# Turning the attention's output by transposing DMAs from two fp16 parts, instead of by TensorE from fp32

## The chip, the cores and the metric

One Trainium2 chip, of which the kernel uses one core. The metric is the device time of one execution in microseconds (us); lower is better. Engines are called as in the profile: PE (TensorE) with its weight loads PEld, DVE (VectorE), ACT (ScalarE), POOL (GpSimd), SP (the engine that issues the DMAs; SPq in the timeline).

## The reference

```python
# x: 2048 rows of 640; 32 heads of 20; window of 256
xn = layernorm(x)
q, k, v = split(xn @ wqkv)                      # 640 -> 3 * 640
p = softmax(where(0 <= i - j < 256, q @ k.T * 20 ** -0.5, -1e9))
s = (p @ v) @ wo                                # attention, then the last projection
h = relu(xn @ w1 + b1) ** 2                     # 640 -> 1536
g = silu(h @ w2 + b2)                           # 1536 -> 640
return x + s * g
```

Products are made in fp16: a matrix is split into a high part and a low part (the rounding rest), and three products (high by high, high by low, low by high) are added.

## The kernel before, in words

Three stages. The first normalises x, turns it, makes v and the first q and k. The second is the attention, with the MLP mixed in. The third ("the last stage" here) multiplies the attention's output with wo, by silu of the MLP's output y, and adds x.

The attention is a loop over 269 steps: 16 pairs of heads by 16 query tiles of 128 rows, plus a lag. In each step TensorE makes scores for the maxima (sps, `scores`) and, ten steps later, transposed scores into a PSUM tile of which there is only one (stps, `scores_t`). ACT takes the exponential (p, `exps`), POOL masks it with two selects (L627, L629), ACT makes its high part (ph, `high`), DVE the low part (pl, `low`), and TensorE multiplies both with v (ops, `values`). Every four steps a group of 4 query tiles for one pair of heads is done, 64 groups in all: ACT copies ops out (osb, `normed`), DVE takes a reciprocal (rs), POOL adds two halves (on, L667) and multiplies by rs (L670), and SP stores the result to the DRAM tile of that group of rows (o_0 to o_3). These three parts of `normed` are spread: osb at the end of a step, the addition in the next step, and the multiplication late in that same step.

Into the gaps TensorE gets other work from a generator (`filler`), with a budget per step: q and k of the later pairs, then `hidden_unit` (hps, with relu and hh on ACT, sq on DVE and a subtraction to hh on POOL as its evacuation), `out_unit` (yps, stored to y), and last `out_filler`, the last stage. Evacuations are put in a list and run by `flush()`, once a step.

The order on each engine is that of the program text: the schedule is written out by hand. All DMAs go through SP, one queue, in order; each also waits for the one issued eight places before it. mrow is a small transfer to qs (the maxima's rows, 2 KB), which stps of later steps need.

The last stage has 8 units of 256 rows. `load` brings the unit's rows of o and y back (ob, yb); `transposes` turns ob on TensorE (otp: 10 transposes of 128x128 fp32), ACT and DVE split the result to fp16 parts (oT); then 60 products (wops), their evacuation on DVE (`finish`) and the store. Unit 0's transposes are placed in the attention's last steps, each other unit's inside the unit ahead of it. Large tiles share a pool of ten (`bigp`), used in turn.

Of the kernel before, what the change touches and what calls it, by code (L numbers as in the profile page):

```python
# [7 lines left out]
F32 = mybir.dt.float32  # L8
# [6 lines left out]
P = 128  # L15
S = 2048
D = 640
# [41 lines left out]
def attn_mlp_kernel(ctx: ExitStack, tc, x, wqkv, wo, w1, b1, w2, b2, out):  # L59
# [23 lines left out]

    v_d = dram.tile([P, NP, NB, 4 * 2 * VW], F16, name="v_d")
    y_d = dram.tile([P, NT, D], F32, name="y")
    o_d = [dram.tile([4, P, D], F32, name=f"o_{g}") for g in range(NB)]


    ident = const.tile([P, P], F32, name="ident")
# [568 lines left out]
    def normed(p, g):  # L658
        ot = ots.pop((p, g))
        osb = at2.tile([P, 8, VW], F32, tag="osb", name="osb")  # L660
        nc.scalar.activation(osb, ot.rearrange("p a h w -> p (a h) w"), AF.Copy)

        def rest():
            rs = at2.tile([P, 8], F32, tag="rs", name="rs")
            nc.vector.reciprocal(rs, osb[:, :, VW - 1])
            on = at2.tile([P, 8, DH], F32, tag="on", name="on")
            nc.gpsimd.tensor_add(on, osb[:, :, 0:DH], osb[:, :, DH:2 * DH])  # L667

            def last():
                nc.gpsimd.tensor_mul(on, on, rs.unsqueeze(2).to_broadcast([P, 8, DH]))  # L670
                post(o_d[g].rearrange("t p d -> p t d")[:, :, 2 * DH * p:2 * DH * (p + 1)], on.rearrange("p (t h) d -> p t (h d)", t=4))
            norm.append(last)
        return rest


    early = at2.tile([P, 1], F32, tag="early", bufs=1, name="early")
    state = [0.0, 0.0, 0]
# [2 lines left out]
    def post(dst, src):  # L680
        posts.append((dst, src))
# [12 lines left out]
    def flush(upto=None):  # L694
        for f in late[:]:
            f()
        late.clear()
        while pending and (upto is None or flushed[0] < upto):
            flushed[0] += 1
            pending.pop(0)()  # L700
# [214 lines left out]
    def filler():  # L915
        groups = [(group_unit, g, b, w) for g in range(1, KC) for b in range(NB) for w in "qk"]
        hid = [[(hidden_unit, n, fc) for fc in range(NF)] for n in range(nblk)]
        mlp2 = [[(out_unit, n, tt, nh, third) for tt in range(2) for nh in range(2) for third in range(3)] for n in range(nblk)]
        first = 3 * NB
        units = groups[:first] + merge(groups[first:], hid[0])  # L920
        for n in range(nblk - 1):
            units += merge(hid[n + 1], mlp2[n])
        units += mlp2[-1]
        for u in units:
            if u == (hidden_unit, 1, 2):
                out_scales()
            if u[:3] == (hidden_unit, nblk - 1, 0):
                wo_part = queue_wo()
                shut.add("o")
            if u[:2] == (out_unit, nblk - 1):  # L930
                shut.discard("o")
                load(0)
                load(1)
            if u == (out_unit, nblk - 1, 1, 1, 1) and 0 in ld:
                yield from transposes(0)
            yield from u[0](*u[1:])
        ensure("o")
        yield from out_filler(wo_part)

    ld = {}  # L940

    def ready(u):
        return state[2] >= NP * NT - NT + 4 * (u // 2) + 3 + LAG + 5

    def load(u):
        if u in ld or u >= 2 * NB or not ready(u):
            return
        if u % 2 == 0:
            obs[u // 2] = [bigp.tile([P, KC * BT], F32, tag="big", name=f"{w}_{u // 2}").rearrange("p (u t d) -> p u t d", u=2, t=2) for w in ("ob", "yb")]
        ob, yb = (t_[:, u % 2] for t_ in obs[u // 2])  # L950
        t0 = 2 * (u % 2)
        nc.sync.dma_start(ob, o_d[u // 2][t0:t0 + 2].rearrange("t p d -> p t d"))
        nc.sync.dma_start(yb, y_d[:, 2 * u:2 * u + 2, :])
        ld[u] = (ob, yb)

    obs = {}

    def queue_wo():
        wob = [bigp.tile([P, SLOT], F16, tag="big", name=f"wo{j}") for j in range(2)]
        for c in range(KC):  # L960
            hi, lo = (lin1(wob, (2 * c + q) * D, D) for q in range(2))
            piece("o", wo[c * P:(c + 1) * P, :], lambda raw, hi=hi, lo=lo: split_s(hi, lo, raw, mlp["so"]))
        return lambda p, c: lin1(wob, (2 * c + p) * D, D)

    oT = {}

    def transposes(u):
        ob = ld[u][0]
        oT[u] = bigp.tile([P, SLOT], F16, tag="big", name=f"oT_{u}")[:, :SLOT // 2].rearrange("p (s c n) -> p s c n", s=2, c=KC)
        for c0 in range(0, KC, 2):  # L970
            cs = range(c0, min(c0 + 2, KC))
            flush(mark() - 2)
            if state[2] < 10 ** 6:
                ps = pmm.tile([P, len(cs), MT], F32, tag="mm", name="otp")
            else:
                if c0 == 2:
                    ps = pst.tile([P, 2, 4 * P], F32, tag="st", name="otp")[:, 0, :].rearrange("p (c n) -> p c n", n=MT)
                else:
                    ps = pat.tile([P, len(cs), MT], F32, tag="s", name="otp")
            for c in cs:  # L980
                for t in range(2):
                    nc.tensor.transpose(ps[:, c - c0, t * P:(t + 1) * P], ob[:, t, c * P:(c + 1) * P], ident)  # L982
                    yield 0.12

            def evac(ps=ps, c0=c0, n=len(cs)):
                split(oT[u][:, 0, c0:c0 + n], oT[u][:, 1, c0:c0 + n], ps)
            pending.append(evac)

    def out_filler(wo_part):
        xts = {}  # L990

        def load_res(t):
            xts[t] = wgt.tile([P, D], F32, tag="wraw", bufs=RAW, name="xres")
            nc.sync.dma_start(xts[t], x[t * P:(t + 1) * P, :])

        def finish(ps, sl, t2, nh, res, xt, t, yb):
            nc.vector.scalar_tensor_tensor(res[:, sl], ps, mlp["io"], yb[:, t2, sl], ALU.mult, ALU.mult)
            nc.vector.tensor_add(res[:, sl], res[:, sl], xt[:, sl])
            if t == NT - 1:
                post(out[t * P:(t + 1) * P, sl], res[:, sl])  # L1000
            elif nh:
                post(out[t * P:(t + 1) * P, :], res)

        load_res(0)
        for u in range(2 * NB):
            while u not in ld:
                load(u)
                if u not in ld:
                    yield None
            load(u + 1)  # L1010
            if u not in oT:
                yield from transposes(u)
            flush()
            yb = ld[u][1]
            nc.scalar.activation(yb, yb, AF.Silu)
            for t2 in range(2):
                t = 2 * u + t2
                xt = xts.pop(t)
                res = wgt.tile([P, D], F32, tag="ysb", name="res")
                for nh in range(2):  # L1020
                    if t2 and not nh and u + 1 in ld:
                        yield from transposes(u + 1)
                    sl = slice(nh * HALF, (nh + 1) * HALF)
                    cuts = [sl] if (t, nh) != (NT - 1, 1) else [slice(HALF, HALF + HALF // 2), slice(HALF + HALF // 2, D)]
                    for sl in cuts:
                        ps = pmm.tile([P, HALF], F32, tag="mm", name="wops")[:, 0:sl.stop - sl.start]
                        mms = []
                        for c in range(KC):
                            for op, wp in ((0, 0), (0, 1), (1, 0)):
                                mms.append((oT[u][:, op, c, t2 * P:(t2 + 1) * P], wo_part(wp, c)[:, sl]))  # L1030
                        yield from mm_group(ps, mms, 0.138)
                        if sl is not cuts[-1]:
                            pending.append(lambda ps=ps, sl=sl: finish(ps, sl, t2, nh, res, xt, t, yb))
                    if nh == 0 and t + 1 < NT:
                        load_res(t + 1)
                    load(u + 1)
                    load(u + 2)

                    pending.append(lambda args=(ps, sl, t2, nh, res, xt, t, yb): finish(*args))
# [17 lines left out]
    with tc.manual_schedule(engines={E_.PE, E_.Activation, E_.DVE, E_.Pool, E_.SP}):  # L1057
# [5 lines left out]
        for s in range(steps):  # L1063
# [34 lines left out]
                maxima(*a, sc)  # L1098
            if rows:
                rows()  # L1100
            if norm:
                norm.pop()()
            if b:
# [9 lines left out]
                high(*c, *exs.pop(c))  # L1113
            while norm:
                norm.pop()()
            fill((1 - EARLY_FILL) * per + SWING * (-1) ** (s - LAG - 3))
            if e and e[1] % 2:
                values(e[0], e[1] - 1)
# [2 lines left out]
                    norm.append(normed(e[0], e[1] // 4))  # L1121
        while norm:
            norm.pop()()
        state[2] = 10 ** 6
        for _ in fl:
            post_all()
# [26 lines left out]
```

## Time and profile before

| | |
|---|---|
| median of 3 runs | 824.12 us (823.79 to 825.47) |
| the profiled execution | 825.52 us, of which the span of the instructions is 823.8 us |
| granted TensorE clock | 1.00 |
| busy: PE, DVE, ACT, POOL | 812.3, 688.8, 646.6, 481.7 us |
| DMA | 104.51 MB, queue q1 40.9% of 16 engines' span |

A line of the timeline has the start in us, the length in us, the engine, the line of the kernel, the operation, out<-in, the shapes; in brackets the idle time before it and what ended it. A line of the stretches has the stretch and its length, then the busy us (and instructions) of PE, PEld, DVE, ACT and POOL, the granted clock, the DMA engines' mean busy share, and GB/s. Matmuls overlap, so their lengths add up to more than the time they take.

### The profile page before, as it was taken

How to read it: one execution, taken by the hardware profiler on the slowest of the kernel's cores; microseconds unless marked ns; L12 is line 12 of the kernel's file. 1: busy time of each engine (PE TensorE's matmuls, PEld its weight loads, DVE VectorE, ACT ScalarE, POOL GpSimd, SP SyncE). 2: the span in 40 equal slices, each digit the busy share in tenths (PEclk: the TensorE clock that was granted, in tenths of full speed). 3: DMA queues.
4: the chain of work that ended last, by engine and by line, in shares of the span. 5: the costliest groups of instructions: out<-in, count | busy, mean ns of one | idle time of the engine just before them, and what ended most of it. 6: DMA issues, size and time to landing. Idle time of an engine off the chain costs nothing.

```text
span 823.8 us, 24953 instructions
## 1 busy us (share of the span) xinstructions
PE 812.3 (99%) x9453; PEld 546.3 (66%) x9453; DVE 688.8 (84%) x1903; ACT 646.6 (78%) x1024; POOL 481.7 (58%) x874
## 2 busy tenths in 40 slices
PE   8999999999999999999999999999999999999998
PEld 7775563455555567777777777777777777767776
DVE  6777566888899999899989999899998999975665
ACT  5466455999899989898989989899998989893321
POOL 2000000566587788787878878888887879760000
PEclk9999999999999999999999999999999999999999
DMA  6895357764654621121222222122132231056883
GB/s 243 248 343 159 127 165 246 225 179 122 185 153 141 181 89 51 51 67 39 66 67 56 67 57 67 36 70 66 35 80 56 75 83 47 26 186 201 295 293 130
DMA packets 100641, 104.51 MB, mean 127 GB/s; under 512 B 42536, under 2 KB 73000, under 8 KB 100520
## 3 DMA queue, kind: packets, MB, share of 16 engines
q1 hardware_dynamic: 100520, 102.91, 40.9%
q8 instruction: 74, 1.21, 0.7%
q14 instruction: 47, 0.39, 0.2%
HBM read 65.67 MB, written 36.83 MB: 124 GB/s over the span
## 4 chain that ended last, share of the span: by engine, by line
PE 89%; ACT 4%; DVE 3%; DMA 2%; issue 1%; SPq 1%; POOL 0%; ACTq 0%; DVEq 0%; POOLq 0%
PE hps L705 20%; PE yps L901 19%; PE qkps L705 11%; PE ops L654 8%; PE wops L705 8%; PE sps L574 8%; PE vps L293 6%; PE stps L621 4%; PE qkps L519 3%; DMA raw<-in_A_wqkv_dram 1%; PE otp L982 1%; ACT p L626 1%; DMA wvr<-in_A_wqkv_dram 1%; PE tps L257 1%; ACT ph L634 1%
## 5 line engine op out<-in xcount | busy, mean ns | idle before, releaser
L626 ACT ACTIVATE p<-stps,ebias,esc 128x768 f32<-128x768 f32 (+2 forms) x256 | 242.2, 946 | 39.5 <-PE stps L621 32.8
L585 DVE CUSTOM_DVE_ANT_0 junk<-sps,mask 128x320 bf16<-128x320 f32 (+2 forms) x512 | 221.3, 469 | 45.7 <-PE sps L574 36.5
L640 DVE TENSOR_TENSOR pl<-p,ph 128x768 f16<-128x768 f32 (+2 forms) x256 | 245.7, 960 | 3.5 <-ACT ph L634 2.0
L627 POOL TENSOR_SCALAR_AFFINE_SELECT p<-p 128x256 f32<-128x256 f32 x256 | 174.5, 682 | 77.2 <-ACT p L626 73.6
L634 ACT ACTIVATE ph<-p 128x768 f16<-128x768 f32 (+2 forms) x256 | 203.0, 793 | 3.0 <-POOL p L629 3.0
L705 PE MATMUL hps<-xT,w 128*128 128x256 f16 x1440 | 189.5, 273 | 0.7 <-ACT relu L875 0.7
L901 PE MATMUL yps<-w,hh 128*128 128x320 f16 x1152 | 187.3, 300 | 0.0
L705 PEld LDWEIGHTS <-w 128*128 128x128 f16 x1440 | 132.4, 98 | 44.9 <-issue 25.4
L901 PEld LDWEIGHTS <-hh 128*128 128x128 f16 x1152 | 104.8, 98 | 56.2 <-issue 22.6
L705 PE MATMUL qkps<-xT,qkw 128*128 128x512 f16 x480 | 115.4, 380 | 0.0
L629 POOL TENSOR_SCALAR_AFFINE_SELECT p<-p 128x256 f32<-128x256 f32 x224 | 109.9, 491 | 0.0
L654 PE MATMUL ops<-vp,ph 128*128 128x41 f16 x1440 | 89.8, 181 | 0.0
L654 PE MATMUL ops<-vp,pl 128*128 128x41 f16 x1440 | 89.5, 180 | 0.0
L654 PEld LDWEIGHTS <-ph 128*128 128x128 f16 x1440 | 84.6, 96 | 5.1
L574 PE MATMUL sps<-ks,qs 60*64 60x320 f16 (+2 forms) x1024 | 84.0, 313 | 2.6 <-DVE mt L585 2.3
L654 PEld LDWEIGHTS <-pl 128*128 128x128 f16 x1440 | 78.9, 96 | 5.1
L590 POOL CAST mp<-mt 128x8 f16<-128x8 f32 x64 | 44.7, 698 | 57.9 <-DVE mt L585 57.4
L621 PE MATMUL stps<-qs,ks 62*64 62x320 f16 (+4 forms) x1024 | 77.5, 290 | 0.6 <-ACT p L626 0.4
L705 PEld LDWEIGHTS <-qkw 128*128 128x128 f16 x480 | 42.5, 98 | 53.7 <-issue 11.5
L879 POOL TENSOR_TENSOR hh<-sq,hh 128x256 f16<-128x256 f32 x96 | 67.2, 700 | 14.2 <-DVE sq L878 8.1
L293 PE MATMUL vps<-wv,xT 128*128 128x320 f16 x480 | 69.6, 299 | 1.3 <-DVE xT L267 0.4
L705 PE MATMUL wops<-wo,oT 128*128 128x320 f16 (+1 forms) x495 | 66.7, 295 | 0.0
(152 smaller groups left out, 977.9 us busy)
## 6 DMA issues: line engine op xcount, KB each, us to landing
raw<-in_B_w_dram SPq DMA_DIRECT2D x24, 320.0 KB
ks<-k_d SPq DMA_DIRECT2D x64, 120.0 KB
qs<-q_d SPq DMA_DIRECT2D x64, 120.0 KB
v_d<-vt SPq DMA_DIRECT2D x8, 656.0 KB
vp<-v_d SPq DMA_DIRECT2D x16, 328.0 KB
xt<-in_A_x_dram SPq DMA_DIRECT2D x16, 320.0 KB
k_d<-shm SPq DMA_DIRECT2D x20, 256.0 KB
q_d<-shm SPq DMA_DIRECT2D x20, 256.0 KB
```

Source lines behind the costliest of these rows:

```text
L293: nc.tensor.matmul(ps, xT[b][:, xp, c, t * P:(t + 1) * P], wv[wp][:, c, nh * HALF:(nh + 1) * HALF], start=n == 0, stop=n == 3 * KC - 1)
L574: nc.tensor.matmul(ps[HB * j:HB * (j + 1), :nk], qs[i][rows_, q0:q0 + HB], ks[i][rows_, k0:k0 + nk], start=True, stop=True)
L585: nc.vector.tensor_tensor_reduce(out=junk[:, :nk], in0=ps[:, :nk], in1=mk, scale=1.0 / MAX_UNIT, scalar=-3.0e38, op0=ALU.add, op1=ALU.max, ...
L621: nc.tensor.matmul(ps[HB * j:HB * (j + 1), hh, c0:c1], ks[i][rows_, kb * P + HB * j:kb * P + HB * (j + 1)], qs[i][rows_, kb * P + c0:kb * ...
L626: nc.scalar.activation(p32[:, :, :n], ps[:, :, :n], AF.Exp, scale=esc[0], bias=ebias)
L627: nc.gpsimd.affine_select(p32[:, :, 0:P], p32[:, :, 0:P], pattern=[[0, 2], [1, P]], compare_op=ALU.is_ge, fill=0.0, base=0, channel_multip ...
L629: nc.gpsimd.affine_select(p32[:, :, 2 * P:], p32[:, :, 2 * P:], pattern=[[0, 2], [-1, P]], compare_op=ALU.is_gt, fill=0.0, base=0, channel ...
L634: nc.scalar.activation(ph[:, :, :n], p32[:, :, :n], AF.Copy)
L640: nc.vector.tensor_sub(pl[:, :, :n], p32[:, :, :n], ph[:, :, :n])
L654: nc.tensor.matmul(ot[:, q % 4, hh, :], t[:, hh, (q - k) * P:(q - k + 1) * P], vp[:, k // 4, k % 4, hh, :], start=m == 1, stop=m == 2 * le ...
L705: nc.tensor.matmul(ps, a, b_, start=j == 0, stop=j == n - 1)
L901: nc.tensor.matmul(ps, hh[:, hp, tt * P:(tt + 1) * P], lin1(w2t, (2 * fc + wp) * D + nh * HALF, HALF), start=fc == 0 and j == 0, stop=fc = ...
```

## The change

The DRAM tiles for the attention's output become fp16, with a high part and a low part. After POOL's multiplication a group is put in a list (`halves`). In the next step, ahead of `exps`, ACT copies it to fp16 (onp, `halves_high`); later in that step DVE makes the low part (`halves_low`), and two stores follow instead of one. In the last stage, `load` issues two transposing DMAs for a unit (one for each part), straight to oT; `transposes` and its evacuations are gone. y's rows are loaded by `load_y`: those of units 0 to 3 at the first `hidden_unit` of the last block, 4, 5 and 6 in the last `out_unit`s, and 7 at the last stage's start. x's rows are loaded two tiles ahead instead of one.

```diff
-    o_d = [dram.tile([4, P, D], F32, name=f"o_{g}") for g in range(NB)]
+    o_d = [dram.tile([2, BT, D], F16, name=f"o_{g}") for g in range(NB)]
...
             def last():
                 nc.gpsimd.tensor_mul(on, on, rs.unsqueeze(2).to_broadcast([P, 8, DH]))
-                post(o_d[g].rearrange("t p d -> p t d")[:, :, 2 * DH * p:2 * DH * (p + 1)], on.rearrange("p (t h) d -> p t (h d)", t=4))
+                halves.append((on.rearrange("p a d -> p (a d)"), g, p))
             norm.append(last)
...
+    def halves_high():
+        on, g, p = halves.pop()
+        parts = at2.tile([P, 2, 8 * DH], F16, tag="onp", name="onp")
+        nc.scalar.activation(parts[:, 0], on, AF.Copy)
+        return on, parts, g, p
+
+    def halves_low(on, parts, g, p):
+        nc.vector.tensor_sub(parts[:, 1], on, parts[:, 0])
+        for s in range(2):
+            post(o_d[g][s].rearrange("(t p) d -> p t d", p=P)[:, :, 2 * DH * p:2 * DH * (p + 1)], parts[:, s].rearrange("p (t d) -> p t d", t=4))
...
             if u[:3] == (hidden_unit, nblk - 1, 0):
                 wo_part = queue_wo()
+                for y in range(4):
+                    load_y(y)
...
-            if u == (out_unit, nblk - 1, 1, 1, 1) and 0 in ld:
-                yield from transposes(0)
...
     def load(u):
...
-        nc.sync.dma_start(ob, o_d[u // 2][t0:t0 + 2].rearrange("t p d -> p t d"))
-        nc.sync.dma_start(yb, y_d[:, 2 * u:2 * u + 2, :])
...
+        for s in range(2):
+            nc.sync.dma_start_transpose(oT[u][:, s], o_d[u // 2][s, u % 2 * MT:(u % 2 + 1) * MT, :])
...
-                    if t2 and not nh and u + 1 in ld:
-                        yield from transposes(u + 1)
...
             if rows:
                 rows()
+            turned = halves_high() if halves else None
             if norm:
                 norm.pop()()
...
             while norm:
                 norm.pop()()
+            if turned:
+                halves_low(*turned)
```

On ACT, the 53rd of the 64 groups (in the profile before it begins at 648.81 us), from osb on. In brackets stands what an instruction waits for. Before:

```order
L661 ACTIVATE osb_13422<-ops_13305 128x328 [waits PE_49]
L626 ACTIVATE p32_13445<-stps_1667,ebias_113,esc_904 128x768 [waits DVE_49,PE_49]
L634 ACTIVATE ph_13457<-p32_13378 128x768 [waits Activation_49,Pool_49]
L626 ACTIVATE p32_13485<-stps_1667,ebias_113,esc_904 128x768 [waits DVE_49,PE_49,Activation_49]
L875 ACTIVATE relu_13499<-hps_13384,m_2_1304,m_0_1302 128x256
```

Now:

```order
L661 ACTIVATE osb_13630<-ops_13511 128x328 [waits PE_49]
L626 ACTIVATE p32_13653<-stps_1667,ebias_113,esc_904 128x768 [waits DVE_49,PE_49]
L634 ACTIVATE ph_13665<-p32_13586 128x768 [waits Activation_49,Pool_49]
L681 ACTIVATE onp_13692<-on_13651 128x160 [waits DMAHW7_49,DMAHW6_49,Pool_49]
L626 ACTIVATE p32_13694<-stps_1667,ebias_113,esc_904 128x768 [waits DVE_49,PE_49,Activation_49]
```

onp stands between ph and the next p, and waits for POOL. POOL's order in the same group, now (before, the same instructions in the same order):

```order
L667 TENSOR_TENSOR on_13651<-osb_13630 128x160 [waits Activation_49]
L627 AFFINE_SELECT p32_13653<-p32_13653 128x2x128 [waits Activation_49]
L629 AFFINE_SELECT p32_13653<-p32_13653 128x2x128
L670 TENSOR_TENSOR on_13651<-on_13651,rs_13649 128x160 [waits DVE_49,Pool_49]
L627 AFFINE_SELECT p32_13694<-p32_13694 128x2x128 [waits Activation_49]
```

The multiplication that onp reads comes behind the two selects of the p one step earlier. On SP in the last stage, before, around the loads of unit 4:

```order
L994 DMA xres_15831<-in_A_x_dram 128x640 [waits DMAHW5_49]
L952 DMA ob_2_15833<-o_2_81 128x2x640 [waits DMAHW6_49,PE_49]
L953 DMA yb_2_15834<-y_78 128x1280 [waits DMAHW7_49,PE_49]
L685 DMA out_0_dram<-res_15813 128x640 [waits DMAHW0_49,DVE_49]
L994 DMA xres_15893<-in_A_x_dram 128x640 [waits DMAHW1_49]
```

Now:

```order
L698 DMA out_0_dram<-res_15976 128x640 [waits DMAHW5_49,DVE_49]
L976 DMA_TRANSPOSE oT_2_16039<-o_2_81 128x5x256 [waits DMAHW6_49,PE_49]
L976 DMA_TRANSPOSE oT_2_16039<-o_2_81 128x5x256 [waits DMAHW7_49]
L992 DMA xres_16058<-in_A_x_dram 128x640 [waits DMAHW0_49]
L698 DMA out_0_dram<-res_16021 128x640 [waits DMAHW1_49,DVE_49]
```

Two transposing DMAs stand where one load of o and one of y stood.

More of the change, by code (lines that the diff above doesn't have):

```diff
@@ L670, in last @@
                 nc.gpsimd.tensor_mul(on, on, rs.unsqueeze(2).to_broadcast([P, 8, DH]))
-                post(o_d[g].rearrange("t p d -> p t d")[:, :, 2 * DH * p:2 * DH * (p + 1)], on.rearrange("p (t h) d -> p t (h d)", t=4))
+                halves.append((on.rearrange("p a d -> p (a d)"), g, p))
             norm.append(last)
         return rest
+    halves = []
+    def halves_high():
[7 more added lines that the diff above has]
+            post(o_d[g][s].rearrange("(t p) d -> p t d", p=P)[:, :, 2 * DH * p:2 * DH * (p + 1)], parts[:, s].rearrange("p (t d) -> p t d", t=4))
     early = at2.tile([P, 1], F32, tag="early", bufs=1, name="early")
@@ L933, in filler @@
                 load(1)
-            if u == (out_unit, nblk - 1, 1, 1, 1) and 0 in ld:
-                yield from transposes(0)
+                load_y(4)
+                load_y(5)
+            if u == (out_unit, nblk - 1, 1, 1, 2):
+                load_y(6)
             yield from u[0](*u[1:])
@@ L938, in filler, with load_y @@
         yield from out_filler(wo_part)
-    ld = {}
+    obs, ybs = {}, {}
     def ready(u):
-        return state[2] >= NP * NT - NT + 4 * (u // 2) + 3 + LAG + 5
+        return state[2] >= NP * NT - NT + 4 * (u // 2) + 3 + LAG + 6
+    def load_y(u):
+        if u not in ybs and u < 2 * NB:
+            if u % 2 == 0:
+                obs["y", u // 2] = bigp.tile([P, KC * BT], F32, tag="big", name=f"yb_{u // 2}").rearrange("p (u t d) -> p u t d", u=2, t=2)
+            ybs[u] = obs["y", u // 2][:, u % 2]
+            nc.sync.dma_start(ybs[u], y_d[:, 2 * u:2 * u + 2, :])
     def load(u):
-        if u in ld or u >= 2 * NB or not ready(u):
+        if u in oT or u >= 2 * NB or not ready(u):
             return
         if u % 2 == 0:
-            obs[u // 2] = [bigp.tile([P, KC * BT], F32, tag="big", name=f"{w}_{u // 2}").rearrange("p (u t d) -> p u t d", u=2, t=2) for w in ("ob", "yb")]
-        ob, yb = (t_[:, u % 2] for t_ in obs[u // 2])
-        t0 = 2 * (u % 2)
-        nc.sync.dma_start(ob, o_d[u // 2][t0:t0 + 2].rearrange("t p d -> p t d"))
-        nc.sync.dma_start(yb, y_d[:, 2 * u:2 * u + 2, :])
-        ld[u] = (ob, yb)
-    obs = {}
+            obs["o", u // 2] = bigp.tile([P, SLOT], F16, tag="big", name=f"oT_{u // 2}").rearrange("p (u s c n) -> p u s c n", u=2, s=2, c=KC)
+        oT[u] = obs["o", u // 2][:, u % 2]
+        for s in range(2):
+            nc.sync.dma_start_transpose(oT[u][:, s], o_d[u // 2][s, u % 2 * MT:(u % 2 + 1) * MT, :])
+    oT = {}
     def queue_wo():
@@ L963, in queue_wo @@
         return lambda p, c: lin1(wob, (2 * c + p) * D, D)
[L965 to L987, printed above, removed]
     def out_filler(wo_part):
@@ L1004, in out_filler @@
         load_res(0)
+        load_res(1)
         for u in range(2 * NB):
-            while u not in ld:
+            while u not in oT:
                 load(u)
-                if u not in ld:
+                if u not in oT:
                     yield None
+            if u == 0:
+                flush()
+                post_all()
+                load_y(7)
             load(u + 1)
-            if u not in oT:
-                yield from transposes(u)
             flush()
-            yb = ld[u][1]
+            yb = ybs[u]
             nc.scalar.activation(yb, yb, AF.Silu)
@@ L1033, in out_filler @@
                             pending.append(lambda ps=ps, sl=sl: finish(ps, sl, t2, nh, res, xt, t, yb))
-                    if nh == 0 and t + 1 < NT:
-                        load_res(t + 1)
+                    if nh and t + 2 < NT:
+                        load_res(t + 2)
                     load(u + 1)
@@ L1123, in attn_mlp_kernel @@
             norm.pop()()
+        halves_low(*halves_high())
         state[2] = 10 ** 6
```

## The prediction, as it was put on record

> **What bounds the kernel now.** I read the page's busy line first, then the chain of waits, then the stretches, then single rows of the timeline. The page and two stretches of the span:
>
> ```profile
> span 823.8 us, 24953 instructions
> PE 812.3 (99%) x9453; PEld 546.3 (66%) x9453; DVE 688.8 (84%) x1903; ACT 646.6 (78%) x1024; POOL 481.7 (58%) x874
> ...
> L626 ACT ACTIVATE p<-stps,ebias,esc 128x768 f32<-128x768 f32 (+2 forms) x256 | 242.2, 946 | 39.5 <-PE stps L621 32.8
> ...
> L621 PE MATMUL stps<-qs,ks 62*64 62x320 f16 (+4 forms) x1024 | 77.5, 290 | 0.6 <-ACT p L626 0.4
> ```
> ```profile
> 300.00:700.00 400.00, 399.31 (x5584) 286.20 (x5583) 366.25 (x1080) 365.52 (x556) 335.33 (x588) 1.00 0.23 61
> ...
> 752.00:808.00 56.00, 56.00 (x427) 42.48 (x426) 35.20 (x68) 15.48 (x25) 0.00 (x0) 1.00 0.80 286
> ```
>
> PE is busy throughout, and in all 256 steps stps waits for ScalarE only 0.4 us: TensorE is the bound. But in the attention (second fence; the columns are PE, weight loads, DVE, ACT, POOL) ScalarE works 365.5 of 400 us and VectorE 366.3. ScalarE has 34.5 us idle. A group of four steps lasts about 9.1 us there (44 groups in the 400 us), so its spare time is 0.78 us a group, most of it waiting for TensorE. The bound and the runner-up lie 9% apart.
>
> The last stage, in the chain of waits (start, length, what):
>
> ```profile
> 751.64 1.09 PE otp L982 x10
> 752.73 8.15 PE wops L705 x60
> ...
> 807.09 1.09 PE otp L982 x10
> ```
>
> There, each unit of 256 rows costs TensorE 1.09 us of transposes and 8.15 us of products, back to back.
>
> **Removed: 80 TensorE transposes with their 24 evacuations.** Seven units stand in the chain with 1.09 us each: 7.6 us. Unit 0's transposes lie at the end of the attention:
>
> ```profile
> 738.96 1.67 PE L901 MATMUL yps<-w,hh 128*128 128x320 f16 x11
> 740.47 0.60 PE L982 MATMUL otp<-ident,ob 128*128 128x128 f32 x4
> ...
> 742.66 0.44 PE L982 MATMUL otp<-ident,ob 128*128 128x128 f32 x2 [0.72 <-DVE oT L123]
> 742.93 0.43 PE L901 MATMUL yps<-w,hh 128*128 128x320 f16 x2
> ```
>
> From 740.47 to 742.93 TensorE does nothing else, and waits between pieces. At least 1.09 us goes, at most the 2.46 us. I take 1.7, the middle, since the products behind it need ScalarE and VectorE too, which the evacuations also held up. Gain: 7.6 + 1.7 = 9.3 us. The evacuations of the other units cost nothing now: ScalarE is busy 15.5 of 56 us there.
>
> **Added: a ScalarE copy in each of 64 groups, with a wait.** This decides. The copy of the normalised output (onp) is the first ScalarE instruction of its step, ahead of that step's exponential p, and it reads what POOL's multiplication (L670) writes. Nothing on ScalarE waited for that multiplication before; only a store did. ScalarE works in order, so p stands behind it; the next step's stps waits for p, because there is one stps buffer; and TensorE's whole queue stands behind stps. A group of before, in which ScalarE evacuates nothing in between:
>
> ```profile
> 650.01 0.84 ACT L634 ACTIVATE ph<-p 128x768 f16<-128x768 f32 x1
> 650.92 0.99 ACT L626 ACTIVATE p<-stps,ebias,esc 128x768 f32<-128x768 f32 x1
> ...
> 650.92 0.40 POOL L629 TENSOR_SCALAR_AFFINE_SELECT p<-p 128x256 f32<-128x256 f32 x1
> 651.30 0.45 POOL L670 TENSOR_TENSOR on<-on,rs 128x160 f32<-128x160 f32 x1
> ...
> 651.77 0.37 SPq L685 DMA_DIRECT2D o<-on  x1
> ...
> 652.77 0.31 PE L621 MATMUL stps<-qs,ks 62*64 62x320 f16 x4
> ```
>
> ScalarE would reach the copy at 650.85, the multiplication ends at 651.75 (the store behind it starts at 651.77, which confirms a POOL row that might be rough), so ScalarE waits 0.90 us. For the copy itself I use the nearest row: an evacuation of 256 elements took 0.38 us and of 512 0.60, so 160 take 0.30:
>
> ```profile
> L122 ACT ACTIVATE oT<-otp x24: 383/592/597, 741.1 to 808.6; 128x512 f16<-128x512 f32 x16, 128x256 f16<-128x256 f32 x8
> L123 DVE TENSOR_TENSOR oT<-otp,oT x24: 415/682/692, 741.9 to 809.4; 128x512 f16<-128x512 f32 x16, 128x256 f16<-128x256 f32 x8
> ```
>
> Then p starts at 652.05 and not 650.92, ends at 653.04, and stps, due at 652.77, is 0.27 us late. Now a group with an evacuation (relu, hh), where POOL has the subtraction of hh ahead of the multiplication:
>
> ```profile
> 641.55 0.83 ACT L634 ACTIVATE ph<-p 128x768 f16<-128x768 f32 x1
> 642.28 0.97 ACT L626 ACTIVATE p<-stps,ebias,esc 128x768 f32<-128x768 f32 x1
> ...
> 642.51 0.67 POOL L879 TENSOR_TENSOR hh<-sq,hh 128x256 f16<-128x256 f32 x1
> 643.14 1.17 POOL L670 TENSOR_TENSOR on<-on,rs 128x160 f32<-128x160 f32 x1
> ...
> 644.33 0.39 SPq L685 DMA_DIRECT2D o<-on  x1
> ...
> 643.60 0.31 PE L621 MATMUL stps<-qs,ks 62*64 62x320 f16 x4
> ```
>
> ScalarE is free at 642.38, the multiplication ends at 644.31: 1.93 us of waiting. p would start at 644.61 and end at 645.58, and stps, due at 643.60, would be 1.98 us late.
>
> I did the same for all groups in the step loop but the last two, 62 in all; the first and the last of them (multiplication, p, next stps):
>
> ```profile
> 160.56 0.45 POOL L670 TENSOR_TENSOR on<-on,rs 128x160 f32<-128x160 f32 x1
> 161.24 1.00 ACT L626 ACTIVATE p<-stps,ebias,esc 128x768 f32<-128x768 f32 x1
> 162.57 0.31 PE L621 MATMUL stps<-qs,ks 62*64 62x320 f16 x4
> ...
> 734.16 0.45 POOL L670 TENSOR_TENSOR on<-on,rs 128x160 f32<-128x160 f32 x1
> 732.87 0.99 ACT L626 ACTIVATE p<-stps,ebias,esc 128x768 f32<-128x768 f32 x1
> 734.63 0.33 PE L621 MATMUL stps<-qs,ks 62*64 62x320 f16 x4
> ```
>
> The first costs TensorE 0.09 us, the last 1.27. Over the 62: ScalarE waits 78.7 us (1.27 a group), p is late by 86.6 us, its lead over stps takes up 0.79 us a group, and TensorE is late by 43.2 us: 34.1 in the 29 groups with an evacuation or weight split, 9.1 in the other 33.
>
> That sum lets ScalarE win its whole lead back before the next group. The other bookkeeping says it can't quite: per group 1.27 of waiting + 0.30 of copying - 0.78 of spare time = 0.79 us, times 62 = 49 us. I take the middle, 46 us. Low end: in 26 groups the multiplication took over 0.6 us where 0.45 is its usual time, presumably beside VectorE; were it 0.45 everywhere, the 43.2 would be 28.7. High end: if only 0.5 us of the spare time a group can be used, 1.07 x 62 = 66 us.
>
> **Added on VectorE:** 64 subtractions (low parts) of 160 elements, 0.32 us each by the row of oT above (0.42 at 256, 0.68 at 512). VectorE's spare time is 33.8 us over the 44 groups, 0.77 a group, and the new step is longer than the old one: nothing on the path. The last group's copy and subtraction feed only unit 6, some 45 us later: nothing.
>
> **Stores and SP.** Each group's one store of 160-byte pieces becomes two of 80-byte pieces, the first waiting for ScalarE, the second for VectorE, where one waited for POOL. Behind them on SP stand the next pair's q, k and v loads and the two rows of maxima; they come about a step later (2.25 us) and are needed several steps after they are issued. One more issue costs SP 0.37 us a group. The DMA engines were 23% busy in the attention; even a doubling of that leaves them free. Zero, with up to 2 us for a late row of maxima. Below nothing isn't possible: nothing is taken off the queue.
>
> **y loaded sooner.** Four loads of 640 KB at the start of the last hidden block, two more at the last outer units, are moved past mrow's two small transfers and past wo's pieces. 2.6 MB at the 286 GB/s of the second stretch is 9.2 us of queue once, against some three steps (6.8 us) that a row of maxima has: zero to 2.4 us; I take zero, because the steps get longer. The x rows, two ahead instead of one, cost nothing: a unit's products cover them.
>
> **The transposing DMAs.** The trace has none; the nearest row is the plain load of the same bytes.
>
> ```profile
> o<-on SPq DMA_DIRECT2D x64, 80.0 KB
> ...
> ob<-o SPq DMA_DIRECT2D x8, 640.0 KB
> ```
>
> Before, a unit moved ob, yb, x and out, 640 KB each, in 9.24 us at a DMA share of 0.80: 7.4 us, 1.85 for each part. After, yb is gone: 3.7 us for x and out, and the two transposing DMAs may take 4.45 us before they exceed the 8.15 us of products. That is 2.4 times the plain price; I take the plain price, so they are hidden. They are issued a unit or more (8 us) ahead, which covers their latency. The low end is zero too, since TensorE's products remain.
>
> The Trainium skill's page "DMA: Bandwidth & Descriptors", section "Latency and other measured facts", gives 261 GB/s for DMA transposes; by that, as an estimate, a unit's two take 2.5 us, and the sum would stay as it is. The Trainium skill's page "VectorE: DVE Perf Modes", section "The three transpose paths", gives 1309 ns for one 128x128 block through the DMA and 390 ns through TensorE; if a unit's 20 blocks went one after the other that would be, as an estimate, 26 us, and the change would lose in the last stage as well. No row here shows either.
>
> **Sum.** The profiled execution took 825.5 us (span 823.8), 1.4 us over the runs' median of 824.1. 825.5 - 9.3 + 46 = 862.2; against the median 860.8. I say 861 us, 4.5% slower.
>
> **Rivals.**
> *Faster: the wait costs TensorE nothing.* The place is ScalarE's wait ahead of p; it decides by how much later than now p ends compared with stps. The gain of 9.3 us is used up at 0.15 us of lateness a group. Taking 1.0 us off p's lateness in every group still leaves 11.2 us, so the multiplication would have to come over a microsecond sooner. For it: stps waited 0.4 us in all, and some POOL spans are rough. Against it: the stores start 0.02 us after those ends, and the POOL instructions ahead are in the same order. Then only the gain is left: 814.8, say 815 us.
> *Slower still: transposing DMAs bind the last stage.* At four times the plain price, 7.4 us, a unit takes 11.1 us instead of 8.15; over 6 units that is 18 us more, 879 us. For it: the share was 0.80 already. Against it: a quarter of the bytes leaves the stage, and lateness of 2.4 times is allowed.
> *The change doesn't do what it says:* the transposes and evacuations do go, and no other TensorE work replaces them; this one I drop.
>
> **From this to numbers.** The base is the 814.8 us of the gain alone. Likeliest case, 0.71: 814.8 plus 28.7 to 66 gives 843.5 to 880.8. Transposing DMAs binding as well, 0.11: 862 to 899 (18 us on top). The wait half hidden, 0.03: 826 to 843. Faster, 0.13: around 815. Within 0.2%, about what a measurement of this kernel can tell from no change (1.6 us), 0.02. A range of 835 to 885 leaves out the faster case, the middle one and half of the second. Faster 0.13, same 0.02, slower 0.71 + 0.11 + 0.03 = 0.85.
>
> **What would show it.** In the profile after: ScalarE's onp with about 1.3 us of idle time ahead of it, released by POOL's multiplication, some 80 us in all; stps with 40 us or more of idle time released by p; groups of some 9.8 us instead of 9.1; units of the last stage 8.15 us apart with no gaps. I am wrong if stps still waits next to nothing, or if wops waits for oT.

## The result and the profile after

The changed kernel takes 889.71 us in the median (885.44 to 893.54); before took 824.07 us beside it. The profiled execution took 890.26 us. The ratio is 1.0794 (95% interval 1.077 to 1.0819): 7.9% slower, 65.6 us. The forecast was 861 us with a range of 835 to 885: the right direction, and too little by 29 us. The four executions differ with the mean granted clock, from 885.44 us at 0.994 to 893.54 at 0.986.

The same parts of the page as before (span, busy time, and the two groups of the attention that wait for each other, with the new copy):

```profile
span 888.5 us, 25050 instructions
PE 823.5 (93%) x9373; PEld 547.4 (62%) x9373; DVE 693.1 (78%) x1943; ACT 646.0 (73%) x1064; POOL 468.1 (53%) x874
...
L626 ACT ACTIVATE p<-stps,ebias,esc 128x768 f32<-128x768 f32 (+2 forms) x256 | 241.0, 941 | 10.9 <-PE stps L621 6.9
...
L621 PE MATMUL stps<-qs,ks 62*64 62x320 f16 (+4 forms) x1024 | 79.4, 295 | 50.2 <-ACT p L626 49.1
...
L681 ACT ACTIVATE onp<-on 128x160 f16<-128x160 f32 x64 | 21.5, 336 | 92.5 <-POOL on L670 92.5
```

Before, p's line was:

```profile
L626 ACT ACTIVATE p<-stps,ebias,esc 128x768 f32<-128x768 f32 (+2 forms) x256 | 242.2, 946 | 39.5 <-PE stps L621 32.8
```

TensorE fell from 99% busy to 93%. Of the idle times, stps waiting for p rose from 0.4 to 49.1 us, p waiting for stps fell from 32.8 to 6.9 us (ScalarE's lead is nearly used up), and the new copy waits 92.5 us for POOL's multiplication. The stretch of the attention, in the columns explained above (PE, PEld, DVE, ACT, POOL, clock, DMA share, GB/s):

```profile
300.00:700.00 400.00, 366.54 (x4941) 259.11 (x4940) 336.36 (x994) 329.46 (x531) 289.95 (x519) 1.00 0.24 54
```

No engine is the bound there any more: TensorE is busy 366.5 us of 400, VectorE 336.4, ScalarE 329.5. They take turns. One group, with an evacuation, in the timeline:

```profile
675.71 0.84 ACT L634 ACTIVATE ph<-p 128x768 f16<-128x768 f32 x1
...
677.25 1.15 POOL L670 TENSOR_TENSOR on<-on,rs 128x160 f32<-128x160 f32 x1
...
678.43 0.34 ACT L681 ACTIVATE onp<-on 128x160 f16<-128x160 f32 x1 [1.89 <-POOL on L670]
678.67 0.97 ACT L626 ACTIVATE p<-stps,ebias,esc 128x768 f32<-128x768 f32 x1
...
679.70 0.33 PE L621 MATMUL stps<-qs,ks 62*64 62x320 f16 x4 [1.25 <-ACT p L626]
```

Read it downwards: ScalarE is done with ph at 676.55 and then stands for 1.89 us in front of the copy, until the multiplication ends at 678.40; p starts only then, and TensorE stands for 1.25 us in front of the next stps. Averaged over groups 16 to 59, a group lasts 10.23 us instead of 9.08.

Where the 64.7 us of span lie is told by the first and the last product of the last stage, before and after:

```profile
L705 PE MATMUL wops<-wo,oT x495: 232/299/299, 746.8 to 820.2; 128*128 128x320 f16 x155, 128*128 128x160 f16 x10
```
```profile
L718 PE MATMUL wops<-wo,oT x495: 232/299/471, 811.2 to 884.9; 128*128 128x320 f16 x155, 128*128 128x160 f16 x10
```

The first product comes 64.4 us later (811.2 - 746.8): that is the attention. From there to the end of the span it takes 77.3 us instead of 77.0, though the 7.6 us of transposes of units 1 to 7 are gone. So the last stage lost 7.9 us as well. The longest product, 471 ns instead of 299, is the first hint at why. The stretches around it:

```profile
826.00:831.20 5.20, 0.19 (x2) 0.00 (x0) 0.57 (x2) 0.00 (x0) 0.00 (x0) 0.89 1.05 290
...
831.20:833.20 2.00, 2.00 (x8) 1.14 (x8) 1.93 (x5) 0.00 (x0) 0.00 (x0) 0.50 1.12 206
833.20:835.20 2.00, 2.00 (x10) 1.07 (x8) 0.45 (x1) 0.00 (x0) 0.00 (x0) 0.50 1.04 249
835.20:836.20 1.00, 1.00 (x5) 0.55 (x4) 0.77 (x2) 0.00 (x0) 0.00 (x0) 0.50 1.03 410
836.20:837.20 1.00, 1.00 (x6) 0.64 (x5) 0.27 (x1) 0.00 (x0) 0.00 (x0) 0.67 0.67 264
837.20:838.20 1.00, 1.00 (x10) 0.71 (x8) 0.00 (x0) 0.00 (x0) 0.00 (x0) 1.00 0.84 279
```

TensorE stops for 5.0 us (826.2 to 831.2), and then has a granted clock of 0.50 for some 5.7 us. The products that start between 831.2 and 842.3 are one line:

```profile
831.20 11.34 PE L718 MATMUL wops<-wo,oT 128*128 128x320 f16 x62 [5.01 <-DVE res L995]
```

At 8.15 us for 60 products, 62 would have taken 8.58 us from the first start to the last end (61 distances of 0.136 us, and 0.30 us for the last): 2.76 us less. From the start of the last product ahead of the stop (825.89) to the start of the next one it is 5.31 us instead of 0.14, so the stop costs 5.17. 5.17 + 2.76 = 7.93 us, which is the whole loss. What TensorE waited for stands on SP, where all DMAs are issued in order:

```profile
809.71 0.45 SPq L967 DMA_DIRECT2D yb<-y  x1
810.21 0.90 SPq L992 DMA_DIRECT2D xres<-in_A_x_dram  x2
811.94 0.33 SPq L698 DMA_DIRECT2D y<-ysb  x1
819.21 0.33 SPq L967 DMA_DIRECT2D yb<-y  x1
819.63 0.94 SPq L698 DMA_DIRECT2D o<-onp  x2
820.62 4.11 SPq L976 DMA_TRANSPOSE oT<-o  x2
824.77 0.58 SPq L992 DMA_DIRECT2D xres<-in_A_x_dram  x1
825.45 0.38 SPq L698 DMA_DIRECT2D out_dram<-res  x1
```
```profile
SPq L967 <- DMA y<-ysb: 6.9, 1, 6.9
...
DVE res L995 <- DMA out_dram<-res: 9.2, 1, 9.2
...
PE wops L718 <- DVE res L995: 5.0, 1, 5.0
```

The chain, from cause to end: the last rows of y are stored at 811.94 and land 7 us later, behind 640 KB of y and two tiles of x that were put on the queue just ahead (809.71, 810.21). Unit 7's y load (load_y(7), L967) reads these rows, so SP waits 6.9 us in front of it. Everything behind is late, the transposing DMAs and the first store of the output among them; SP spends another 4.1 us (820.62 to 824.73) on issuing two transposing DMAs ahead of that store. The store lands 5 us after its issue. VectorE has two res buffers and waits 9.2 us for that store; TensorE needs the PSUM tile that VectorE would have emptied.

The Trainium skill's page "TensorE: Matmul & The Clock Gate", section "Part 1: The HAM clock gate (the "warmup" mystery)", states a half clock after about 3.4 us of idleness and a full one after as long of work, by a window that runs freely. The trace agrees on the half (0.50 after this stop); the way back took 5.7 us of work here. It doesn't agree on the idleness: the changed kernel's clock was halved twice in the attention too, where no wait at stps was over 1.8 us. Each time some 3.41 us of half clock follow on 3.41 us in which TensorE was busy for about half (the column behind the length):

```profile
249.78:253.19 3.41, 1.86 (x36) 1.21 (x35) 1.09 (x4) 2.09 (x4) 2.05 (x4) 1.00 0.31 75
253.19:256.60 3.41, 3.41 (x16) 0.95 (x13) 3.29 (x9) 2.67 (x4) 1.44 (x4) 0.50 0.33 28
...
410.20:413.61 3.41, 1.66 (x29) 1.20 (x27) 3.13 (x9) 1.54 (x3) 2.09 (x4) 1.00 0.52 155
413.61:417.03 3.42, 3.42 (x18) 1.93 (x14) 1.55 (x2) 2.90 (x5) 3.19 (x7) 0.50 0.31 64
```

The second of them lies in the stretch of 400 us above, whose mean of 1.00 hides it by rounding.

### The profile page after: what moved, and what is told of

The parts are those of the page before. It is cut to its first block, busy times and chain, and to the rows that moved or that the text cites. A ratio compares the mean times of both kernels' runs of the same rounds, so it can differ in the third digit from the quotient of the medians.

```text
span 888.5 us, 25050 instructions
## 1 busy us (share of the span) xinstructions
PE 823.5 (93%) x9373; PEld 547.4 (62%) x9373; DVE 693.1 (78%) x1943; ACT 646.0 (73%) x1064; POOL 468.1 (53%) x874
## 4 chain that ended last, share of the span: by engine, by line
PE 47%; ACT 19%; POOL 15%; DVE 9%; issue 7%; DMA 2%; SPq 1%; DVEq 0%; ACTq 0%; POOLq 0%
ACT p L626 11%; PE yps L914 7%; PE hps L718 7%; PE qkps L718 7%; PE wops L718 6%; PE vps L293 5%; POOL p L627 5%; POOL on L670 4%; PE sps L574 3%; ACT ph L634 3%; PE ops L654 3%; PE qkps L519 3%; PE stps L621 3%; POOL hh L892 2%; POOL p L629 2%
## 5 line engine op out<-in xcount | busy, mean ns | idle before, releaser
L627 POOL TENSOR_SCALAR_AFFINE_SELECT p<-p 128x256 f32<-128x256 f32 x256 | 152.3, 595 | 139.4 <-ACT p L626 136.7
L621 PE MATMUL stps<-qs,ks 62*64 62x320 f16 (+4 forms) x1024 | 79.4, 295 | 50.2 <-ACT p L626 49.1
L629 POOL TENSOR_SCALAR_AFFINE_SELECT p<-p 128x256 f32<-128x256 f32 x224 | 105.6, 471 | 0.0
L681 ACT ACTIVATE onp<-on 128x160 f16<-128x160 f32 x64 | 21.5, 336 | 92.5 <-POOL on L670 92.5
L891 DVE TENSOR_TENSOR sq<-relu 128x256 f32<-128x256 f32 x96 | 53.7, 560 | 37.4 <-ACT relu L888 37.0
L621 PEld LDWEIGHTS <-ks 62*64 62x64 f16 x1024 | 37.7, 105 | 64.3 <-issue 63.5
```

Of the source, the lines that this page charges most:

```text
L621: nc.tensor.matmul(ps[HB * j:HB * (j + 1), hh, c0:c1], ks[i][rows_, kb * P + HB * j:kb * P + HB * (j + 1)], qs[i][rows_, kb * P + c0:kb * ...
L627: nc.gpsimd.affine_select(p32[:, :, 0:P], p32[:, :, 0:P], pattern=[[0, 2], [1, P]], compare_op=ALU.is_ge, fill=0.0, base=0, channel_multip ...
L629: nc.gpsimd.affine_select(p32[:, :, 2 * P:], p32[:, :, 2 * P:], pattern=[[0, 2], [-1, P]], compare_op=ALU.is_gt, fill=0.0, base=0, channel ...
```

## The experiments

Theories: **A**, ScalarE's in-order wait for POOL ahead of p costs nearly all of the attention's loss. **B**, a good part of it is something else that the change adds: VectorE's subtractions, the doubled stores, SP. For the last stage: **C**, unit 7's y load stops SP; **D**, the transposing DMAs bind it.

**1. The copy later in its step.** From the changed kernel:

```diff
-            turned = halves_high() if halves else None
             if norm:
 ...
             flush()
             tick()
+            turned = halves_high() if halves else None
             if c:
                 high(*c, *exs.pop(c))
```

> The same work as the changed kernel on every engine; only ScalarE's copy onp is moved within its step, from ahead of p to behind the evacuations, where POOL's multiplication has long ended. If ScalarE's wait for POOL is what lengthened the attention (64.4 us up to the first wops): that wait falls from 92.5 us to under 10, stps waits under 5 us, the first wops comes at 745 to 752 us, and the whole takes 820 to 830 us, since the 8 us lost at the start of the last stage stay. If the added work itself (21.5 us of copies, 64 subtractions, twice the stores with half the size) is what lengthened it: 870 us or more.

**2. The multiplication sooner**, right behind the addition on POOL, with the copy where the change has it:

```diff
-            def last():
-                nc.gpsimd.tensor_mul(on, on, rs...)
-                halves.append((on..., g, p))
-            norm.append(last)
+            nc.gpsimd.tensor_mul(on, on, rs...)
+            halves.append((on..., g, p))
```

> ScalarE's copy stays ahead of p as in the changed kernel; POOL's multiplication is issued right behind the addition, ahead of the two selects of p, and so ends sooner. If the wait for POOL is the cause: its 92.5 us fall to under 10 and the time is 820 to 835 us, a little above the version with the copy moved because the selects come 0.45 us later in every fourth step. If the copy's place ahead of p (its 0.34 us, 64 times) or the added work is the cause: 870 us or more.

The copy behind p: 831.46 us, ratio 1.0094 (1.0079 to 1.0109), a little above its band. The early multiplication: 826.85 us, ratio 1.0035 (1.0023 to 1.0047), inside it. One line of text moved gives 58 us back, and another 63. The waits of the first, then (one line) of the second:

```profile
ACT onp L681 <- POOL on L670: 24.9, 28, 1.6
...
ACT p L626 <- DVE pl L640: 8.6, 16, 0.9
...
PE wops L718 <- DVE res L995: 4.2, 1, 4.2
...
PE stps L621 <- ACT p L626: 2.3, 3, 1.7
```
```profile
ACT onp L678 <- POOL on L668: 25.7, 42, 1.5
```

In both the wait ahead of the copy falls from 92.5 to about 25 us, not to under 10 as expected, and stps' wait falls from 49.1 to 2.3 us in the first and 2.1 in the second. The first product of the first run comes at 753.5, a little behind its band of 745 to 752. The first has a new small wait beside it, p for VectorE's pl (8.6 us), which may be what it is slower by. A holds. In both, TensorE still stops in the last stage (4.2 and 3.8 us), so that is a matter of its own.

**3. The copy alone, in the kernel before.** The fp32 store and TensorE's transposes stay; ScalarE makes a copy that nothing reads:

```diff
                 post(o_d[g]..., on...)
+                halves.append(on.rearrange("p a d -> p (a d)"))
 ...
+    def halves_high():
+        onp = at2.tile(...)
+        nc.scalar.activation(onp, halves.pop(), AF.Copy)
 ...
+            if halves:
+                halves_high()
             if norm:
```

> The kernel before, with TensorE's transposes, the fp32 store and no subtraction; added is only ScalarE's copy ahead of p, as the changed kernel has it, into a tile that nothing reads. If the copy with its wait is the whole cause: the attention is longer by 55 to 66 us and the time is 879 to 890 us. If the subtractions or the doubled stores carry a good part: below 865 us. If a copy is just 21.5 us of work in ScalarE's idle time: 824 to 835 us.

881.13 us, ratio 1.0696 (1.0671 to 1.0721). 63 copies of 0.34 us, 21 us of ScalarE's time, cost 57.3 us. Here too the time goes with the mean clock, from 878.80 us at 1.000 to 883.96 at 0.994 (the profiled one, with three halvings in the attention), so the execution at full clock was 55 us above before.

```profile
ACT onp L680 <- POOL on L670: 82.9, 62, 2.7
...
PE stps L621 <- ACT p L626: 40.6, 46, 1.8
```
```profile
L712 PE MATMUL wops<-wo,oT x495: 232/299/299, 805.2 to 878.6; 128*128 128x320 f16 x155, 128*128 128x160 f16 x10
```

The first product is 58.4 us late, of the 64.4 of the changed kernel. This settles A's size, to the few us that the clock adds. What is left for B in the attention is 6 us, and 8 if unit 0's transposes, which the changed kernel saves and run 3 doesn't, are worth about 2.

**4. Unit 7's y load later**, on top of run 1:

```diff
                 post_all()
-                load_y(7)
             load(u + 1)
+            if u == 2:
+                load_y(7)
```

> As the version with the copy moved, and the last load of y (unit 7) is issued in unit 2 of the last stage instead of at its start, where it waits for the store of the last y rows and holds up all DMAs behind it. If that wait made TensorE stop in the last stage (5.0 us, and about 2.9 us at a lower clock behind it): 7 to 9 us below the version with the copy moved, 812 to 820 us, with no gap in wops. If the transposing DMAs themselves are too slow at the stage's start: within 2 us of it.

825.11 us, ratio 1.0012 (1.0003 to 1.0022): 6.35 us below run 1, slightly less than the 7 to 9 expected. The absolute number is missed because the attention itself still ends 6.5 us later than before (first product at 753.3). The products now follow each other without a gap:

```profile
755.13 64.39 PE L718 MATMUL wops<-wo,oT 128*128 128x320 f16 x486
```

C is shown: nothing else was moved, and the stop and the half clock are both gone. Moved with the load are its wait and its 640 KB, so this run doesn't tell which of the two counts; the trace above has the wait in the chain. SP is as busy with two transposing DMAs here as in the changed kernel (4.45 us from 758.30), and TensorE doesn't stop.

**5. The early multiplication with the late y load** (runs 2 and 4 together).

> Two edits together: POOL's multiplication right behind the addition, and unit 7's y loaded in unit 2 of the last stage. If the two losses are separate, their savings add: 826.9 less the 6.4 us by which the late load alone improved the version with the copy moved, 820.5 us (818.5 to 822.5), 0.4% below the kernel before. If one hides behind the other: 824 us or more.

821.28 us, ratio 0.998 (0.996 to 1.0), as expected: the two edits add up, and the changed kernel stands where the one before stood.

**6. Without the subtractions**, from run 5:

```diff
-        nc.vector.tensor_sub(parts[:, 1], on, parts[:, 0])
 ...
-            post(..., parts[:, s]...)
+            post(..., parts[:, 0]...)
```

> As the version with both edits, but VectorE's 64 subtractions are left out and the high part is stored in both places, so the low part is missing from the output. Without the wait the attention is still 3 us (first wops 749.9 against 746.8) longer than before, where 1.7 us less had been forecast. If VectorE, then 93% busy, is what costs it: first wops at 746 to 748 us, 2 to 4 us faster than with the subtractions. If it is ScalarE's copies or the doubled stores: within 1 us of that version.

This one stores the high part twice. 815.1 us, ratio 0.9897 (0.9884 to 0.991): 6.2 us below run 5, more than the 2 to 4 expected. VectorE in the attention, run 5 and then this one (third number of the busy columns):

```profile
300.00:700.00 400.00, 398.18 (x5514) 286.28 (x5513) 373.96 (x1110) 367.52 (x591) 340.71 (x580) 1.00 0.28 67
```
```profile
300.00:700.00 400.00, 398.91 (x5572) 286.00 (x5568) 366.33 (x1077) 372.66 (x598) 331.64 (x586) 1.00 0.29 67
```

VectorE falls from 374.0 to 366.3 us of 400. It was never full, and having the subtractions still costs about 6 us of B. Two things went with them: VectorE's work, and the second store's wait for it on SP. The doubled stores stayed, and the first product comes earlier than before (744.4 against 746.8), so they cost nothing that shows.

**7. Plain loads in place of the transposing ones**, from run 5:

```diff
-            nc.sync.dma_start_transpose(oT[u][:, s], o_d[u // 2][s, ...])
+            nc.sync.dma_start(oT[u][:, s]..., o_d[u // 2][s, ...].rearrange("(t p) d -> p t d", p=P))
```

> As the version with both edits, with plain loads of the same bytes in place of the 16 transposing DMAs, so the last projection gets rows that are not turned. If the transposing DMAs are hidden behind the products, as the gapless wops say: within 1 us of that version, while the DMA share of the last stage falls from about 0.9 to 0.7 and SP's issue of one from 1.35 to about 0.45 us. If they still cost time: more than 2 us faster.

820.9 us, ratio 0.9963 (0.995 to 0.9977), 0.4 us from run 5. With unit 7's load moved, D is out: the transposing DMAs are hidden. (Whether plain loads alone would have spared the changed kernel its stop, in whose chain 4.1 us of their issue stand, was not run.) They aren't cheap, though. The last stage and the SP rows, with transposing DMAs (run 5) and with plain ones:

```profile
770.00:806.00 36.00, 36.00 (x267) 25.93 (x266) 18.23 (x36) 1.27 (x1) 0.00 (x0) 1.00 1.03 270
```
```profile
L973 SPq DMA_TRANSPOSE oT<-o x16: 1387/1793/3893, 734.4 to 795.6; - x16
```
```profile
770.00:806.00 36.00, 36.00 (x267) 25.93 (x266) 18.34 (x36) 1.27 (x1) 0.00 (x0) 1.00 0.72 241
```
```profile
L973 SPq DMA_DIRECT2D oT<-o x16: 366/480/960, 733.2 to 793.0; - x16
```

TensorE has no gap in either. The DMA share is 1.03 instead of 0.72 (it counts the packets' times, which can overlap), but run 5's stretch also holds part of unit 7's y. From 700 to 820 us both move the same bytes; their queue's packets, MB and share, with transposing DMAs and with plain ones:

```profile
q1 hardware_dynamic: 34656, 20.58, 67.8%
```
```profile
q1 hardware_dynamic: 18016, 20.58, 55.4%
```

As an estimate, 12.4% of 120 us, over 8 units, is 1.9 us more for a unit's two DMAs than the plain 1.85, about twice the plain price; the prediction put break-even at 2.4 times. Not much of the cover is left.

**8. The early multiplication, the late copy and the late y load together.**

> All three edits: POOL's multiplication early, ScalarE's copy late, unit 7's y late. Each of the first two alone left ScalarE 25 us of waiting for POOL; together the copy comes a whole step after the multiplication. If that rest still costs time: the wait is under 3 us and the time 816 to 819.5 us. If ScalarE's rest of waiting lay in idle time and VectorE is the bound: within 1 us of the version with the two edits.

845.27 us, ratio 1.0266 (1.0253 to 1.0278): missed by far. The expectation took the copy to come a whole step after the multiplication. It doesn't: the list is filled early in a step and emptied late in the same one, so the copy has POOL's multiplication of its own step just ahead.

```profile
ACT onp L678 <- POOL on L668: 56.2, 58, 2.0
...
DVE onp L682 <- ACT onp L678: 35.4, 50, 1.5
```
```profile
644.73 1.06 POOL on L668
645.81 0.34 ACT onp L678
646.59 0.48 DVE junk L585
```

In the second fence, the chain of waits runs from POOL over ScalarE's copy to VectorE. It is the same mistake as the change's on one more engine: the subtraction waits 35.4 us for the copy, and VectorE's other work stands behind it.

**9. The copy a step later in truth.** From run 5, the list is looked at when the step begins and emptied late in it:

```diff
-            turned = halves_high() if halves else None
+            due = len(halves)
 ...
             tick()
+            turned = halves_high() if due else None
```

> What the version with all three edits was meant to be: there, the multiplication's new place let the copy follow it in the same step, so ScalarE and behind it VectorE waited for POOL once more (56 and 35 us). Here the copy stands at the late place of the step after the multiplication. If the remaining wait of about 26 us in the version with the two edits costs time: wait under 3 us and 814 to 818 us. If it lay in idle time and VectorE's subtractions are the bound: 819 to 822 us, as the version with the two edits.

**10. As 9, the subtraction on POOL** (`nc.gpsimd.tensor_sub` for `nc.vector.tensor_sub`).

> As the other kernel of this pair, with the 64 subtractions on POOL (some 0.53 us each, by the addition of the same size) instead of VectorE. If the 6 us that leaving them out saved were VectorE's load: 2 to 5 us faster than with them on VectorE, if POOL has room (it is 85% busy). If POOL then delays its selects and with them ScalarE: slower than with them on VectorE by 2 us or more.

Run 9 takes 819.43 us, ratio 0.9943 (0.993 to 0.9957); run 10 takes 818.8 us, ratio 0.9935 (0.9923 to 0.9948). By these intervals the two can't be told apart; both are some 5 us under the kernel before, and the fastest of the versions that compute everything. In 9 the copy's wait is gone:

```profile
ACT onp L678 <- POOL on L668: 2.3, 3, 1.2
```

and still only 1.9 us came back. So 26 us of waiting in run 5 had cost next to nothing: 0.42 us a group and 0.34 for the copy make 0.76, just under ScalarE's spare 0.78. Run 10 missed both of its expectations; the subtraction took 0.81 us on POOL, where VectorE had taken 0.50 in run 9 (means), and moving it gained 0.6 us, no more than the noise. What the 6 us of run 6 consist of is left open by that: leaving the subtractions out frees them, and moving them to the engine with the most spare time doesn't. In both runs 9 and 10 the second store still waits for the subtraction.

## Why the prediction was right in direction and short in size

**The place and the mechanism were right.** The prediction's signs came: onp idle ahead of POOL's multiplication (about 80 us foretold, 92.5 in the changed kernel, 82.9 in run 3), stps with 40 us or more behind p (49.1 and 40.6). Groups were to last 9.8 us and last 10.23.

**The term that failed is "I take the middle, 46 us".** Run 3 measures it at 57.3, and 55 in the one execution at full clock. The prediction had two ways of counting. One let ScalarE win its lead back between groups (43.2); the other took waiting plus copying less spare time, for 62 groups (49). With the sizes of run 3 the second gives 82.9 + 62 x 0.34 - 62 x 0.78 = 55.6 us. So the second was the right sum, and a middle between it and the first was not an estimate of anything: that is 3 of the 11 us. It was also under-sized: the wait by 4.2 us (78.7 against 82.9), presumably since POOL and ScalarE shift against each other once both wait, and the copy by 2.5 us (0.34 against 0.30 us each, read off rows of other widths). The last 1.7 us can be the halved clock, which the prediction didn't reckon with; no run isolates it.

**VectorE's subtractions, "nothing on the path", was wrong by about 6 us** (run 6). The argument was spare time on average, 0.77 us a group against 0.32. In the changed kernel a subtraction does take 0.32 us (0.46 in run 5), so the size was right; that a spare average means no step is late was not. Which steps are late, and whether it is VectorE's load at all or the store that waits for it, isn't shown: with the subtraction on POOL (run 10) the 6 us stay.

**"Zero to 2.4 us; I take zero" for y loaded sooner was wrong by 7.9 us** (run 4: 6.35 us). It weighed the bytes of the early loads and mrow behind them. It counted six of the eight loads and passed over the one that the change puts at the start of the last stage, unit 7's, and so never asked what this one waits for and what stands behind it on SP. By the trace the price was not the bytes but a wait of 6.9 us in an in-order queue, plus 2.8 us of half clock that no row of before shows. These three terms make 11 + 6 + 8 = 25 of the 29 us that were missing.

**The gains came as foretold.** Units follow each other 8.15 us apart in run 4 (one line of 64.39 us without a gap), and its last stage takes 69.6 us (822.9 - 753.3) instead of 77.0, so the 7.6 us are there but for 0.2. For unit 0, run 6's first product stands at 744.4, 2.4 us ahead of 746.8 before, near the upper end (2.46) of the bounds; that is the net of all that run 6 changes in the attention, its copies included.

**The transposing DMAs were hidden, as taken,** at a price of about twice the plain one instead of the plain price assumed. By the Trainium skill's page "DMA: Bandwidth & Descriptors", section "Latency and other measured facts" (261 GB/s with a non-contiguous middle dimension, more without), a unit's two would take 2.5 us or less, as an estimate; run 7 against run 5 puts them near 3.7 us, beside x and output traffic, so slower. By the page "VectorE: DVE Perf Modes" of the Trainium skill, section "The three transpose paths" (1309 ns a block), 20 blocks in turn would make 26 us; the gapless units of 8.15 us exclude that.

**Together**, on the clock of the first product: 58.4 (run 3) + 6.3 (run 6 against run 5: 750.7 - 744.4) - 2.4 (unit 0) = 62.3 of 64.4 us; in the last stage - 7.6 + 7.9 = 0.3 of 0.3 us. 2.1 us are not assigned. The 6.3 and the 2.4 both come from run 6, and their difference is run 5's delay against before (750.7 - 746.8), so the sum checks this difference and not the two parts.

**The rivals.** "The wait costs TensorE nothing" (815 us) is the case of runs 5 and 9, which needed the multiplication more than a microsecond sooner, as its condition said. "Transposing DMAs bind the last stage" (879 us) came close in its number by luck: no product waited for oT, and all that the transposing DMAs have to do with the loss is their 4.1 us of issue in the chain of the one stop.

## What to carry to other kernels

Price a small instruction that reads another engine's result on an engine that works in order as wait plus own time less that engine's spare time, times how often; here a copy of 0.34 us cost 0.9 us each time, and nearly nothing when its producer ran about a microsecond sooner. Don't take the middle of two bookkeepings: decide which holds. For each DMA that is moved on a shared queue, ask what it itself waits for and which transfers stand behind it; one load of 640 KB in the wrong place cost 7.9 us in a stage that otherwise has no gap.

## What the runs showed of the hardware that was not expected

A stop of TensorE costs more than its length: after 5.0 us the granted clock was 0.50 for 5.7 us of work, 2.8 us more on 62 products. It takes no long stop either. In the attention of the changed kernel, with waits of 1.8 us at most, the clock was halved twice for 3.41 us, each time behind 3.41 us in which TensorE was busy for 1.66 and 1.86 us; in run 3 it was three times, behind 1.60 to 1.66 us. Not every stretch as thin does it (1.61 us busy in the 3.41 from 536.5 in the changed kernel, and the clock stays at 1.00), so these traces give no threshold. In the profiled execution of the kernel before, the thinnest 3.41 us behind the first 8 us have TensorE busy for 2.12, and the clock stays at 1.00 to the last product.

A transposing DMA of 320 KB keeps SP 1.79 us (median) where a plain one of the same bytes takes 0.48 (runs 5 and 7), so in an in-order queue it delays its followers even while its own data is early.
